# Hash attention and SwiGLU on one core: the normed x of six units turned by DMA instead of on TensorE, with the feed forward planned four slots later

## The chip, the cores and the metric

The kernel runs on one core of a Trainium2 chip. TensorE (PE) multiplies matrices and also transposes blocks by multiplying with an identity; VectorE (DVE), ScalarE (ACT) and GpSimd (POOL) do the rest; SP issues most of the DMAs. Each engine takes its instructions strictly in the order in which the program gives them, and waits for data of other engines through semaphores. The metric is the device time of one execution in microseconds (us). Lower is better.

## The reference

The first half is attention with a hash mask: a query sees the keys whose six sign bits under a fixed projection equal its own. The second half normalises the rows and feeds them through a gated layer.

```python
B, H, S, D = 4, 8, 768, 64            # batch, heads, sequence, head size
mask   = bucket(q @ proj)[:, :, :, None] == bucket(k @ proj)[:, :, None, :]
scores = where(mask, q @ k.T / sqrt(D), -1e9)
attn   = exp(scores - max); attn = attn / (sum(attn) + 1e-09)
x      = (attn @ v).transpose(0, 2, 1, 3).reshape(3072, 512)
rms    = sqrt(mean(x * x, axis=-1) + 1e-06)
xn     = x / rms * rms_g
g, val = xn @ w_gate, xn @ w_val      # 512 -> 1536 each
out    = (g * sigmoid(g) * val) @ w_out   # 1536 -> 512, float32
```

## The kernel before, in words

**Units and slots.** The 3072 rows are cut into eight units of 384 rows: unit u is half u % 2 of batch u // 2. Attention goes through 192 slots. Slot t issues the scores of step t + 1 (`scores`, line 335, two matmuls), the exponential of step t on ACT (`probs`, line 347), and then whatever a plan holds for that slot. Three slots make one head, 24 slots (`NS`) one unit. Scores lie in two PSUM buffers, so the scores of step t + 2 wait until the exponential of step t is done. Two of each three slots also hold half of the product with v (`av`, line 360).

**After a pair of heads**, `o_step` (lines 374 to 387) puts the pair's output in the float32 tile `x` of the unit: an addition and a reciprocal on DVE, a product on POOL. `s_step` (lines 397, 403) adds up the squares. For unit u of 1 to 6, with t0 = 24 (u + 1), the last pair's `o_step` lies in slot t0 + 2, its `s_step` and the norm in slot t0 + 4. `norm_scale` reduces on DVE (415) and takes the power -1/2 on POOL (419), and `norm_third` (430) multiplies each third of `x`, 128 rows by 512, by the row's factor into the fp16 tile `xn`: three DVE instructions.

**Turning.** The feed forward needs xn with the 512 columns on the partitions. `turn_x` does a third: four PE transposes of 128x128 into a PSUM bank (`x_ps`, 437), and one DVE instruction (443) that writes them to `xnT` and multiplies by the norm's weight, which lies along the partitions there (`gcol`). For the last third of unit 0 and the middle one of unit 7, ACT does this in four instructions (441).

**Feed forward.** For each of 12 blocks of 128 hidden columns there are `gate` and `value`, four matmuls of 384 columns each (454), halved into two pieces. ACT takes a tanh of the gate (462), DVE makes two passes (471, 472) and writes `ht`. `project` (483) multiplies `ht` by `wo` into `y_ps`, `store` (495, 496) copies a third of the output on ACT and sends it off on SP's queue. All PSUM banks of this part (`x_ps`, `g_ps`, `v_ps`, `y_ps`, the hash's `d_ps`) come from one pool of three (`bank`).

**The planner.** `spread(t0, n, pieces)` deals pieces of PE work into n slots, so that the estimated PE time (`PROJ` 216 ns, `FEED` 324, `TURN` 220, with fixed amounts for scores and av) is even over the slots. In the window of unit u, slots t0 to t0 + 23, the pieces are, in this order: nine pieces of four `project` matmuls of unit u - 1, with the three turns of unit u behind the seventh and the eighth, and then 48 halves of gate and value of unit u. Unit 0's gates lie in slots 38 to 47. The hash (`hash_one`) and the means of v have slots of their own and take their share of the time.

**The tail.** After slot 191 nothing of scores is left. A few slots finish the last head (av in slots 193 and 194, the last `o_step` on DVE in slot 194), then `project(6, ...)`, norm(7), three `turn_x(7, ...)`, the gates and values of unit 7 and its projections follow without a planner.

SP's queue carries the loads of q, k and v (105, 119), the hash bits (294) and the stores (496). ACT's queue carries two DMAs in all: one at the start (512) and the very last store (508).

## Time and profile before

| | us |
|---|---|
| median of 2 runs | 331.15 (330.91 to 331.39) |
| the profiled execution: time / span on the chip | 330.52 / 328.7 |
| busy: PE / DVE / ACT / POOL | 323.0 / 239.5 / 227.2 / 158.4 |
| granted TensorE clock | 0.999 |

The span runs from the first to the last instruction; the 1.8 us by which the time exceeds it lie around the program. A busy engine is one that executes instructions; time in which it waits is idle. Instructions that issue a DMA are not counted as busy; they stand in the trace under the engine's queue (SPq, ACTq), with the time that they hold the issuing sequencer. PE's matmuls overlap in the records, so the cost of a PE instruction is read from the distance between the starts of neighbours, not from its own duration.

### The profile page before, as it was taken

The page shows a single profiled execution, that of the slowest core. Times are in us where ns is not written, and L with a number is a line of the kernel's source. Part 1 is how long each engine was busy: PE and PEld are TensorE (multiplying, and loading weights), DVE is VectorE, ACT ScalarE, POOL GpSimd, SP SyncE. Part 2 cuts the span into 40 slices and gives each one's busy share as a digit, 9 for nine tenths or more (in the row PEclk, how much of TensorE's full clock was granted, in tenths as well). Part 3 has the DMA queues.
Part 4 walks back from the last instruction along what each step waited for, and adds up shares of the span by engine and source line. Part 5 has one row for each costly group of instructions (what it writes and reads, how often), then busy time and mean ns, then how long its engine had stood idle before and what let it go on. Part 6 is the DMA issues. An engine that isn't in the chain of part 4 may idle for free.

```text
span 328.7 us, 7869 instructions
## 1 busy us (share of the span) xinstructions
PE 323.0 (98%) x2999; PEld 196.6 (60%) x2999; DVE 239.5 (73%) x526; ACT 227.2 (69%) x331; POOL 158.4 (48%) x204
## 2 busy tenths in 40 slices
PE   8999999999999999999999999999999999999995
PEld 3676666656565566656566565655566566665554
DVE  5887877859888778967888568876768455685860
ACT  7999886766678677775768667785767767744321
POOL 4999759955974542824674521755462111221000
PEclk9999999999999999999999999999999999999999
DMA  7943999988139554432816136001000010002002
GB/s 236 335 158 99 225 211 191 184 157 142 70 58 165 118 114 87 73 77 82 164 21 133 36 93 117 7 3 68 34 5 3 34 64 2 0 2 96 3 1 97
DMA packets 79614, 30.93 MB, mean 94 GB/s; under 512 B 64908, under 2 KB 76632, under 8 KB 79576
## 3 DMA queue, kind: packets, MB, share of 16 engines
q1 hardware_dynamic: 75672, 25.65, 33.2%
q0 software_dynamic: 3680, 4.72, 8.5%
q8 instruction: 23, 0.38, 0.5%
q14 instruction: 15, 0.12, 0.1%
q10 hardware_dynamic: 224, 0.07, 0.1%
HBM read 28.32 MB, written 6.29 MB: 105 GB/s over the span
## 4 chain that ended last, share of the span: by engine, by line
PE 97%; ACT 1%; issue 0%; DVE 0%
PE s_ps L335 20%; PE g_ps L454 19%; PE v_ps L454 19%; PE y_ps L483 18%; PE o_ps L360 11%; PE d_ps L215 2%; PE t_ps L155 2%; PE d_ps L235 2%; PE x_ps L437 2%; PE z_ps L550 1%; ACT psb L347 1%; PE y_ps L502 1%; PE m_ps L319 1%; DVE kT L157 0%; PE s_ps L155 0%
## 5 line engine op out<-in xcount | busy, mean ns | idle before, releaser
L347 ACT ACTIVATE psb<-s_ps,ebias 128x768 f16<-128x768 f32 x192 | 167.7, 899 | 20.8 <-PE s_ps L335 19.9
L335 PE MATMUL s_ps<-QK 128*128 128x384 f16 (+1 forms) x384 | 93.5, 326 | 1.2 <-ACT psb L347 1.1
L462 ACT ACTIVATE t<-g_ps 128x384 f32<-128x384 f32 x96 | 47.1, 491 | 53.0 <-PE g_ps L454 52.9
L454 PE MATMUL g_ps<-xnT,wg 128*128 128x384 f16 x384 | 82.6, 326 | 0.0
L454 PE MATMUL v_ps<-xnT,wv 128*128 128x384 f16 x384 | 81.8, 326 | 0.0
L471 DVE SCALAR_TENSOR_TENSOR a<-t,g_ps 128x384 f32<-128x384 f32 x96 | 52.9, 551 | 27.6 <-ACT t L462 26.0
L381 POOL TENSOR_TENSOR x<-otmp,rcp 128x384 f32<-128x384 f32 x30 | 25.1, 835 | 95.5 <-DVE rcp L379 95.3
L483 PE MATMUL y_ps<-wo,ht 128*128 128x512 f16 x276 | 68.0, 379 | 0.0
L472 DVE SCALAR_TENSOR_TENSOR ht<-a,v_ps 128x384 f16<-128x384 f32 x96 | 53.2, 554 | 11.2 <-PE v_ps L454 2.9
L360 PEld LDWEIGHTS <-psb 128*128 128x128 f16 x1152 | 51.9, 97 | 15.7 <-issue 1.2
L360 PE MATMUL o_ps<-vl,psb 128*128 128x65 f16 x1152 | 55.8, 193 | 0.0
L335 PEld LDWEIGHTS <-QK 128*128 128x128 f16 (+1 forms) x384 | 34.6, 98 | 34.3 <-issue 9.2
L454 PEld LDWEIGHTS <-wv 128*128 128x128 f16 x384 | 35.3, 97 | 21.2 <-issue 0.2
L454 PEld LDWEIGHTS <-wg 128*128 128x128 f16 x384 | 34.8, 97 | 20.8 <-DVE xnT L443 0.4
L483 PEld LDWEIGHTS <-ht 128*128 128x128 f16 x276 | 24.8, 98 | 22.4
L495 ACT COPY ysb<-y_ps 128x512 f32<-128x512 f32 x23 | 13.5, 585 | 19.6 <-PE y_ps L483 19.6
L374 DVE TENSOR_TENSOR otmp<-o_ps,cvb 128x390 f32<-128x390 f32 x32 | 17.8, 557 | 7.6 <-PE o_ps L360 7.6
L207 POOL CAST QK<-qT 64x768 f16<-64x768 f32 x20 | 16.4, 820 | 13.4 <-DVE qT L194 12.8
L430 DVE TENSOR_SCALAR xn<-x,rstd 128x512 f16<-128x512 f32 x23 | 15.8, 738 | 6.8 <-POOL rstd L419 6.8
L387 POOL TENSOR_TENSOR sq<-x 128x384 f32<-128x384 f32 x24 | 19.8, 826 | 1.9
L443 DVE TENSOR_TENSOR xnT<-x_ps,gcol 128x512 f16<-128x512 f16 x22 | 14.5, 686 | 8.0 <-PE x_ps L437 7.9
L207 POOL CAST QK<-kT 64x768 f16<-64x768 f32 x20 | 16.4, 820 | 6.6 <-DVE kT L194 4.7
(83 smaller groups left out, 284.5 us busy)
## 6 DMA issues: line engine op xcount, KB each, us to landing
vn<-in_v_dram SPq DMA_DIRECT2D x16, 384.0 KB
out_dram<-ysb SPq DMA_DIRECT2D x23, 256.0 KB
qL<-in_q_dram SPq DMA_DIRECT2D x40, 96.0 KB
kL<-in_k_dram SPq DMA_DIRECT2D x40, 96.0 KB
kn<-in_k_dram SPq DMA_DIRECT2D x5, 384.0 KB
qn<-in_q_dram SPq DMA_DIRECT2D x5, 384.0 KB
wg<-in_moe_w_gate_dram POOLq DMA_DIRECT2D x2, 768.0 KB, 9.7
wv<-in_moe_w_val_dram POOLq DMA_DIRECT2D x2, 768.0 KB, 11.8
```

Source lines behind the costliest of these rows:

```text
L207: nc.gpsimd.tensor_copy(QK[b, 2 * hp + hh, "h"][0:64, o : o + S], src[64 * hh : 64 * hh + 64, :])
L335: nc.tensor.matmul(ps[:, j, 0:HALF], QK[b, h, "h"][rows, S + jt * 128 : S + (jt + 1) * 128], QK[b, h, "h"][rows, half * HALF : (half + 1) ...
L347: nc.scalar.activation(psb[u, h][:, 2 * ch : 2 * ch + 2, :], sps.pop((u, i))[:, :, 0:HALF], AF.Exp, bias=ebias, scale=ESCALE,)
L360: nc.tensor.matmul(o[:, c, hh, 0:65], psb[u, h][:, jt, c * 128 : (c + 1) * 128], vls[b % 2][:, h, 2 * (jt % 3) + jt // 3 if b in PARITY el ...
L374: nc.vector.tensor_add(tmp[:, :, :, 0:65], o[:, :, :, 0:65], cvb[b % 2][:, 2 * hp : 2 * hp + 2, 0:65].unsqueeze(1).to_broadcast([128, 3, 2 ...
L381: eng.tensor_mul(xd.rearrange("p c (h d) -> p c h d", h=2), tmp[:, :, :, 0:64], r.to_broadcast([128, 3, 2, 64]),)
L387: eng.tensor_mul(sq, xd, xd)
L454: nc.tensor.matmul(ps, w[:, kt, fs], xnT[u][:, kt, :], start=(kt == 0), stop=(kt == 3))
L462: nc.scalar.activation(t, fbank[u, ft, "g_ps"], AF.Tanh, scale=0.5)
L471: nc.vector.scalar_tensor_tensor(out=a, in0=t, scalar=1.0, in1=g, op0=ALU.add, op1=ALU.mult)
L472: nc.vector.scalar_tensor_tensor(out=ht[u][:, ft, :], in0=a, scalar=0.5, in1=vv, op0=ALU.mult, op1=ALU.mult)
L483: nc.tensor.matmul(y, ht[u][:, ft, c * 128 : (c + 1) * 128], wo[:, ft, :], start=(ft == 0), stop=(ft == NF - 1),)
```

## The change

For units 1 to 6 the turn leaves PE. The norm's third becomes one DVE instruction with two tensor operands, which multiplies x by the row's factor and by the norm's weight, laid out along the columns in a new tile `grow` that every partition holds in full. Then `turn_dma` has ACT's queue issue a DMA that transposes the third from `xn` into `xnT`. The three DMAs of a unit lie in slots t0 + 6, t0 + 7 and t0 + 8, behind the exponential of that slot on ACT. `grow` is loaded in slot 3 by SP (one row of 2 KB read for each of 128 partitions) and scaled in slot 41 by ACT. Units 0 and 7 keep `turn_x`.

The planner's windows move by `LAG` = 4 slots: unit 0's gates have slots 38 to 51, and the window of unit u is t0 + 4 to t0 + 27. The window of unit 6 thus ends at slot 195, four slots behind the last scores. The norm's slot does not move.

```diff
+    grow = const.tile([128, DMODEL], FP32, name="grow")
...
+    ONDMA = range(1, 7)
+
+    def turn_dma(u, c):
+        if c == 0:
+            xnT[u] = npool.tile([128, 4, HALF], FP16, name="xnT", bufs=2)
+        nc.scalar.dma_start_transpose(
+            out=xnT[u][:, :, c * 128 : (c + 1) * 128], in_=xn[u][:, c, :]
+        )
...
         for c in range(3 if u else 2):
-            norm_third(u, c, nc.vector.tensor_scalar_mul)
+            if u in ONDMA:
+                nc.vector.scalar_tensor_tensor(
+                    out=xn[u][:, c, :], in0=x[u][:, c, :], scalar=rstds[u][:, c : c + 1],
+                    in1=grow, op0=ALU.mult, op1=ALU.mult,
+                )
+            else:
+                norm_third(u, c, nc.vector.tensor_scalar_mul)
...
+    at(0, 3, nc.sync.dma_start, grow, moe_rms_g.partition_broadcast(128))
+    at(0, 41, nc.scalar.mul, grow, grow, float(DMODEL) ** 0.5)
...
+    LAG = 4
...
-            spread(t0, 2 * NS - t0, gates)
+            spread(t0, 2 * NS + LAG - t0, gates)
             continue
         t0 = NS * (u + 1)
         at(0, t0 + 4, norm, u)
+        for c, s in enumerate((6, 7, 8)):
+            at(0, t0 + s, turn_dma, u, c)
...
-            if i in (6, 7):
-                pieces += [
-                    (TURN, False, [(0, turn_x, u, c)]) for c in ((0,), (1, 2))[i - 6]
-                ]
-        spread(t0, NS, pieces + gates)
+        spread(t0 + LAG, NS, pieces + gates)
```

More of the change, by code (lines that the diff above doesn't have):

```diff
@@ L737 @@
         at(0, t, idle_bank, n)
-    SCORES, AV, PROJ, FEED, TURN, HASH, MEAN = 330, 290, 216, 324, 220, 1000, 120
+    SCORES, AV, PROJ, FEED, HASH, MEAN = 330, 290, 216, 324, 1000, 120
     inserts = {spot[3]: (HASH, hash_one, *pair) for pair, spot in spots.items()}
```

## The prediction

> **What bounds the kernel now.** I read the page's first part, then the chain that ended last, then the stages around the norm of units 1 to 6, one window from slot t0 + 6 on for each, and last the tail.

> ```profile
> PE 323.0 (98%) x2999; PEld 196.6 (60%) x2999; DVE 239.5 (73%) x526; ACT 227.2 (69%) x331; POOL 158.4 (48%) x204
> PE 97%; ACT 1%; issue 0%; DVE 0%
> 73.90:81.00 7.10, 7.10 (x64) 4.36 (x62) 6.95 (x12) 4.79 (x7) 3.26 (x6) 1.00 0.96 164
> 112.00:119.00 7.00, 7.00 (x63) 4.27 (x62) 4.60 (x8) 4.84 (x8) 3.15 (x5) 1.00 0.25 94
> 265.00:272.00 7.00, 6.93 (x69) 4.29 (x68) 3.85 (x7) 4.75 (x7) 1.59 (x2) 1.00 0.19 75
> ```

> The windows' columns are length, then busy PE, PEld, DVE, ACT and POOL, the granted clock, the DMA share and GB/s. PE is busy throughout at full clock, so work taken from PE there shortens the kernel as long as nothing new makes PE wait. ACT has some 2.2 us free in 7. In unit 1's window (73.9) DVE and the DMA engines are nearly full; there the change has least room. The timeline shows the step itself, for unit 2 (slot t0 + 4 starts at 109.32, with the scores that PE issues in it):

> ```profile
> 109.32 0.49 PE L335 MATMUL s_ps<-QK 128*128 128x384 f16 x2
> ...
> 110.03 0.86 POOL L419 TENSOR_TENSOR rstd<-ss,mhalf 128x3 f32<-128x3 f32 x1 [1.05 <-DVE ss L415]
> 110.92 2.76 DVE L430 TENSOR_SCALAR xn<-x,rstd 128x512 f16<-128x512 f32 x3 [0.97 <-POOL rstd L419]
> 111.37 0.90 ACT L347 ACTIVATE psb<-s_ps,ebias 128x768 f16<-128x768 f32 x1 [0.62 <-PE s_ps L335]
> 113.44 0.39 PE L437 MATMUL x_ps<-ident,xn 128*128 128x128 f16 x4
> 113.66 1.03 PE L483 MATMUL y_ps<-wo,ht 128*128 128x512 f16 x4
> 113.86 0.69 DVE L443 TENSOR_TENSOR xnT<-x_ps,gcol 128x512 f16<-128x512 f16 x1 [0.18 <-PE x_ps L437]
> ```

> **What goes.** The four transposes start at 113.44 and the next matmul at 113.66: 0.22 us of PE for a third (0.23 in the tail, 298.96 to 299.19). Eighteen thirds at 0.225 are **-4.05 us**, all on the path. Eighteen evictions at 0.69, 12.4 us, leave DVE; DVE isn't the bound, so I count nothing for them, nor for the three-bank pool having a user less.

> **What comes on DVE.** The third was 0.48 us where POOL is quiet and up to 1.22 beside POOL's casts and additions. No two-operand pass of 512 columns is in the trace. The nearest row is the product x<-otmp,rcp on DVE, 384 columns from two SBUF tensors, 0.557; the 128 further columns add what separates 384 (0.554, L472) from 512 (0.69, L443), so 0.69. Bounds 0.48 to 1.22; a unit's three take 2.1 where they took 1.45 to 2.9. Nothing on the path.

> **What comes on ACT's queue.** Eighteen DMA issues. ACT takes nothing behind one until it is issued, and a DMA waits for its third of xn. Behind it stand the exponentials, and PE's scores wait for those. What an issue costs for a transpose no row shows; rows of issues in the trace:

> ```profile
> L508 ACTq DMA_DIRECT2D out_dram<-ypart x1: 354/354/354, 325.6 to 325.6; - x1
> L512 ACTq DMA_DIRECT2D praw<-in_proj_dram x1: 554/554/554, 0.7 to 0.7; - x1
> L294 SPq DMA_DIRECT2D QK<-bits x80: 659/667/1319, 78.1 to 244.5; - x80
> L119 SPq DMA_DIRECT2D qL<-in_q_dram x40: 561/644/5683, 37.3 to 196.2; - x40
> ```

> (ns: least, median, most.) I call the issue I, from 0.35 to 5.7 us, and take **0.67**, the hash bits, the only transfer from SBUF to SBUF.

> When is the third there? Times are us after the start of slot t0 + 4. Now rstd starts between 0.0 and 1.6. After the change the last gate and value of the unit before lie in slot t0 + 3, so DVE still owes two passes of 0.55 behind a tanh when the slot starts: about 1.3. Then the squares (three of 0.22), the reduction (0.17), the power (0.86): xn's thirds at about 3.8, 4.5 and 5.2, an estimate from these rows. ACT ends the exponential of t0 + 6 at about 2.95 (112.27 in unit 2), so the first DMA waits 0.85 and ends at 3.8 + I. The exponential of t0 + 7 starts at 3.6 now, so it is 0.2 + I late. By the gap in the trace between an exponential's end and the scores that need its buffer, it may be 1.06 to 2.1 late, by unit. With I = 0.67 PE loses nothing. The second and third DMAs end at 3.8 + 2I and 3.8 + 3I where I is above 0.7; the exponentials behind them start at some 5.6 and 7.1 now and have 1.1 to 1.9 and 1.5 to spare. So a unit's stall begins between I = 0.9 and 1.6 and then grows as **3I - 4.8**.

> Landing: PE's first gate of the unit comes behind all nine project pieces: 9 x 0.864, seven scores of 0.325 and nearly five av halves of 0.29, so 11.4. The nearest transfers: the first k tile (192 KB) is issued at 0.73 and used at 3.37, 2.6 us; the last store (64 KB) starts at 325.61 and the span ends at 328.74, 3.1. The last third, issued at 5.2, lands by 5.9 + 3 = 8.9 (I = 0.67), 2.5 before its use. **Nothing**; it costs from a landing of 5.6 us up. POOL's 768 KB loads (9.4 to 11.8) are the upper bound.

> [...] No run here shows a transposing DMA yet.

> **grow.** Its load adds 256 KB behind loads needed much later; nothing. Its scaling is one ACT pass (0.73, L430 on ACT) in a gate slot, where the exponential has 0.5 to spare: **+0.2**.

> **The lag.** It takes no work away, so it matters only where PE's covers change. In slots 38 to 51 PE has less per slot (1.6 us against 2.07); POOL, 16.1 of 16.8 us busy from 47.9 to 64.7, doesn't shrink with it, and may bring x of unit 1 late: **+0.3**. The tail is worse:

> ```profile
> 294.04 0.55 DVE L374 TENSOR_TENSOR otmp<-o_ps,cvb 128x390 f32<-128x390 f32 x1
> ...
> 296.20 0.17 DVE L415 TENSOR_REDUCE ss<-ssp 128x3 f32<-128x15 f32 x1
> 296.46 0.85 POOL L419 TENSOR_TENSOR rstd<-ss,mhalf 128x3 f32<-128x3 f32 x1 [5.53 <-DVE ss L415]
> ```

> Here the last o_step holds DVE 2.13 us (294.04 to 296.17) beside PE's projections of unit 6, which ask nothing new of DVE. With the lag, gates and values 10 and 11 of unit 6 stand around that o_step in slots 194 and 195. PE does value 10 and gate 11 (0.65 each) and then needs a third bank for value 11, the one of gate 10, which DVE frees only behind the o_step and its own pass: 2.13 + 0.55 against 1.3, so **+1.45**. The norm of unit 7 then comes at 5.9 to 6.7, ahead of the turns at 9.5.

> **Sum.** -4.05 + 0.2 + 0.3 + 1.45 = -2.1 us. The profiled execution's 330.52 (span 328.7) becomes 328.4; it lay 0.6 under the median, so **329.0**, for which I give 0.52 (326.7 to 331).

> **Rivals.**
> - *ACT's issue takes the place of PE's turn* (slower). All six units pay 3I - 4.8. It eats the gain at I = 1.7 and makes 2% at about 2.1; I = 2 gives 336, 2.5 gives 345. For it: the qL issues that took up to 5.7 us with the queue loaded, and 0.55 for 1.5 KB on ACT when SP issued in the same instant, against 0.35 alone. Against: medians under 0.7, and SP's string of bits stands behind the norm (unit 1, from 78.06). [...] 0.22.
> - *The landing is late*, PE's first gate waits. Each us beyond 5.6 costs 6: 7 us give 337, 9.4 give 352. For it: 96% DMA share in unit 1's window; against: 0.19 to 0.55 in the other five. 0.14.
> - *The tail costs nothing*, and the evictions' absence helps: -4.05, 327.0, or 326 with a us of small stalls gone. 0.08.
> - *The DMA does not turn in blocks* but moves 2-byte elements: a packet costs 23 ns (33.2% of 16 engines' 328.7 us over 75672), 65536 of them over 16 engines 94 us a third; far over 400. 0.04.

> **Range and chances.** What a measurement tells from no change is about 2%, 324.5 to 337.8 here. Faster than that needs more than the whole PE gain: 0.02. Slower: two thirds of the ACT rival, half of the landing's, the last: 0.26. The rest, 0.72, is same. 326.5 to 341 leaves out the upper ends of both slow rivals and little below.

> **What would show it.** Right: x_ps for units 0 and 7 alone (24 transposes); ACTq issues under a us; no idle of PE at scores or first gates in the six windows; a wait of about 1.4 us of PE on DVE's pass 471 before value 11 near the end. Wrong: PE waiting for psb (ACT rival), or gates waiting on the xnT DMA (landing). The weakest step is I, taken from a plain copy.

## The result and the profile after

| | before | after |
|---|---|---|
| median of 2 runs, us | 331.15 (330.91 to 331.39) | 355.85 (355.66 to 356.04) |
| span of the profiled execution, us | 328.7 | 353.8 |
| granted TensorE clock | 0.999 | 0.981 |

The changed kernel takes 1.0745 times as long (95% interval 1.0727 to 1.0762): 24.7 us more where 2 us less were forecast, and far above the range. The page of the changed kernel, its busy times, the granted clock by slices, and the chain that ended last:

```profile
PE 328.9 (93%) x2926; PEld 194.5 (55%) x2927; DVE 232.5 (66%) x508; ACT 226.6 (64%) x332; POOL 161.3 (46%) x204
...
PEclk9999999996999999999978999999999999999999
...
PE 66%; DVE 11%; POOL 8%; ACT 4%; DMA 3%; issue 3%; SPq 2%; ACTq 1%; DVEq 0%; POOLq 0%
```

PE was 97% of the chain and is 66% now. PE has become busier in spite of 72 transposes less, and the clock line says why: the granted clock is 0.6 in one slice of the span and 0.7 and 0.8 in two neighbouring ones further on. What PE waits for is in its list of waits (engine, line, what it waited for: us in total, times, longest):

```profile
PE s_ps L336 <- DMA QK<-bits: 11.1, 2, 6.5
PE s_ps L336 <- ACT psb L348: 5.6, 12, 1.2
PE v_ps L470 <- DVE a L487: 1.9, 2, 1.6
```

The largest wait is for the hash bits. The change doesn't touch these: they come from the hash through DVE and are sent to their place by SP's queue. Before, no scores waited for them. The waits for exponentials are short, twelve of 0.5 us on average, and the third line is mostly the tail. PE's timeline has the two long waits (start, duration, instruction; in brackets the idle time before it and what ended it):

```profile
84.28 0.80 PE L336 MATMUL s_ps<-QK 128*128 128x384 f16 x2 [4.56 <-DMA QK<-bits]
...
183.07 0.80 PE L336 MATMUL s_ps<-QK 128*128 128x384 f16 x2 [6.51 <-DMA QK<-bits]
```

They are the first scores of the pairs (batch 1, pair 2) and (batch 2, pair 3), steps 60 and 114. The windows of the changed kernel behind them (columns as in the prediction's windows) show that the matter doesn't end with the wait:

```profile
84.20:91.50 7.30, 7.22 (x42) 3.87 (x43) 1.11 (x2) 2.79 (x5) 6.04 (x6) 0.62 0.31 114
91.50:100.00 8.50, 8.50 (x79) 4.97 (x78) 7.04 (x15) 6.00 (x9) 1.66 (x2) 1.00 0.02 5
183.00:190.00 7.00, 6.93 (x41) 3.88 (x42) 2.79 (x6) 2.06 (x4) 0.00 (x0) 0.59 0.44 70
```

In the 7 us behind each wait PE is fully busy, but at 0.62 and 0.59 of its clock, and does 42 and 41 matmuls, where the 8.5 us from 91.5 on, at full clock, hold 79. The clock's records put both stretches at half speed for 6.83 us, from 82.93 and from 181.92, while PE was still idle. Before, where PE has no such wait, they have full speed from 3.65 us to 327.91.

**Why the bits are late.** SP's timeline around the second wait, before:

```profile
136.99 2.65 SPq L119 DMA_DIRECT2D kL<-in_k_dram  x4
...
145.49 5.97 SPq L294 DMA_DIRECT2D QK<-bits  x8
...
164.20 5.98 SPq L294 DMA_DIRECT2D QK<-bits  x8
```

and after:

```profile
145.00 17.43 SPq L120 DMA_DIRECT2D kL<-in_k_dram  x4
...
163.32 7.30 SPq L295 DMA_DIRECT2D QK<-bits  x8
170.66 2.98 SPq L120 DMA_DIRECT2D qL<-in_q_dram  x4
173.75 2.64 SPq L120 DMA_DIRECT2D kL<-in_k_dram  x4
176.49 0.59 SPq L106 DMA_DIRECT2D vn<-in_v_dram  x1
177.19 1.42 SPq L512 DMA_DIRECT2D out_dram<-ysb  x3
178.69 5.97 SPq L295 DMA_DIRECT2D QK<-bits  x8
```

Four loads of a k tile, 2.65 us before, hold SP's queue for 17.4. Then SP issues without a pause and can't catch up: the bits for step 114 are issued at 178.69 in place of 164.20, 14.5 us late, and step 114 comes at 183.07 in place of 169.06, 14.0 late. What SP waited for in the changed kernel:

```profile
SPq L120 <- DMA xnT<-xn: 18.5, 2, 14.9
SPq L295 <- DMA xnT<-xn: 10.8, 4, 8.6
```

| issued at, us | DMA | its semaphore | who had it last, landed at |
|---|---|---|---|
| 144.25 | SP `qL<-in_q_dram`, the fourth | 100 | |
| 145.00 | SP `kL<-in_k_dram` | 104 | |
| 145.63 | SP `kL<-in_k_dram` | 105 | |
| 146.32 | SP `kL<-in_k_dram` | 106 | |
| 159.42 | ACT `xnT<-xn` | 107 | |
| 160.83 | ACT `xnT<-xn` | 109 | |
| 161.87 | SP `kL<-in_k_dram` | 107 | ACT's of 159.42, 161.85 |
| 162.18 | ACT `xnT<-xn` | 103 | |
| 162.53 | SP `vn<-in_v_dram` | 108 | |
| 163.32 | SP `QK<-bits` | 109 | ACT's of 160.83, 163.26 |
| 164.13 | SP `QK<-bits` | 100 | |
| 166.28 | SP `QK<-bits` | 103 | ACT's of 162.18, 166.22 |

So the fourth load of k waits for unit 3's first transpose and the bits for the second and third, and each is issued 0.02 to 0.06 us after the landing. SP reached that place at 147; ACT could issue these transposes only when the norm had made xn, at 159.42, 160.83 and 162.18. A DMA that waits on ACT's queue thus holds SP's queue, 12 us before it is issued itself. Each unit has such a place: unit 1's transposes hold loads of pair (2,0) at 71.66, in front of the bits of step 60 (issued at 81.34, before at 78.06).

**The transposes themselves.** Rows of the timeline for unit 2, whose slot t0 + 4 starts at 114.38 (to be held against the one shown of before):

```profile
116.96 0.86 POOL L429 TENSOR_TENSOR rstd<-ss,mhalf 128x3 f32<-128x3 f32 x1 [1.45 <-DVE ss L425]
117.85 3.56 DVE L438 SCALAR_TENSOR_TENSOR xn<-x,rstd,grow 128x512 f16<-128x512 f32 x3 [0.97 <-POOL rstd L429]
118.56 1.44 POOL L310 TENSOR_TENSOR vadd<-vn 128x384 f32<-128x384 f32 x1
119.18 1.21 ACTq L418 DMA_TRANSPOSE xnT<-xn  x1
120.43 0.90 ACT L348 ACTIVATE psb<-s_ps,ebias 128x768 f16<-128x768 f32 x1 [3.16 <-PE s_ps L336]
120.58 1.20 ACTq L418 DMA_TRANSPOSE xnT<-xn  x1
121.38 0.48 PE L336 MATMUL s_ps<-QK 128*128 128x384 f16 x2 [0.40 <-ACT psb L348]
121.94 1.50 ACTq L418 DMA_TRANSPOSE xnT<-xn  x1
123.27 0.48 PE L336 MATMUL s_ps<-QK 128*128 128x384 f16 x2 [0.27 <-ACT psb L348]
```

The thirds of xn are there 4.8, 6.2 and 7.0 us after the slot's start. ACT stands before the first DMA until then, the exponentials behind it are late, and PE's scores wait 0.3 to 0.4 us for them. (The row at 120.43 puts ACT's idle time down to PE's scores; what ended last was the issue from 119.18 on, which holds ACT to 120.39.) The groups of the new instructions (the first: least, median and most ns; the second: busy us, mean ns, then its idle time):

```profile
L418 ACTq DMA_TRANSPOSE xnT<-xn x18: 1203/1206/1502, 72.8 to 288.0; - x18
L438 DVE SCALAR_TENSOR_TENSOR xn<-x,rstd,grow 128x512 f16<-128x512 f32 x18 | 18.4, 1075 | 5.9 <-POOL rstd L429 5.9
```

**Where the span went.** PE's time, taken from the distances between the starts of neighbouring matmuls (162 ns for an undisturbed one of 384 columns, 216 for 512, 29 for 65, 56 for a transpose; what is above goes to the wait, or, inside a stretch at half clock, to the half clock). Two of the experiments stand beside it:

| us | before | lag alone | units 2, 4, 5, 6 by DMA | after |
|---|---|---|---|---|
| undisturbed work | 299.07 | 299.07 | 296.38 | 294.83 |
| hash matmuls with their waits | 14.09 | 15.36 | 18.10 | 17.03 |
| scores waiting for bits or exponentials | 0 | 1.55 | 5.64 | 18.36 |
| added by the half clock | 0 | 0 | 0 | 5.43 |
| values waiting for a bank, tail included | 0.16 | 5.17 | 5.08 | 2.26 |
| the rest (start, end, small gaps) | 15.42 | 15.59 | 15.02 | 15.93 |
| span | 328.74 | 336.74 | 340.22 | 353.84 |

The trace of the changed kernel lacks the record of one matmul (2926 in place of 2927), so 0.21 us of its undisturbed work stand in another row: 72 transposes at 56 ns are 4.03 us, not the 4.24 between the columns.

### The profile page after: what moved, and what is told of

Its sections match the earlier page's. It is cut to its first block, busy times and chain, and to the rows that moved or that the text cites. A ratio compares the mean times of both kernels' runs of the same rounds, so it can differ in the third digit from the quotient of the medians.

```text
span 353.8 us, 7741 instructions
## 1 busy us (share of the span) xinstructions
PE 328.9 (93%) x2926; PEld 194.5 (55%) x2927; DVE 232.5 (66%) x508; ACT 226.6 (64%) x332; POOL 161.3 (46%) x204
## 4 chain that ended last, share of the span: by engine, by line
PE 66%; DVE 11%; POOL 8%; ACT 4%; DMA 3%; issue 3%; SPq 2%; ACTq 1%; DVEq 0%; POOLq 0%
PE g_ps L470 14%; PE s_ps L336 14%; PE v_ps L470 13%; PE y_ps L499 9%; PE o_ps L361 7%; PE t_ps L156 2%; ACT psb L348 2%; DVE xn L438 2%; DVE a L487 2%; PE d_ps L236 2%; DVE otmp L375 2%; DMA QK<-bits 2%; POOL QK L146 1%; POOL QK L208 1%; PE d_ps L216 1%
## 5 line engine op out<-in xcount | busy, mean ns | idle before, releaser
L336 PE MATMUL s_ps<-QK 128*128 128x384 f16 (+1 forms) x384 | 94.8, 330 | 17.2 <-DMA QK<-bits 11.1
L470 PE MATMUL g_ps<-xnT,wg 128*128 128x384 f16 x384 | 84.7, 331 | 0.2
L499 PE MATMUL y_ps<-wo,ht 128*128 128x512 f16 x276 | 69.0, 382 | 0.0
L470 PEld LDWEIGHTS <-wv 128*128 128x128 f16 x384 | 36.2, 99 | 24.9 <-issue 3.7
L438 DVE SCALAR_TENSOR_TENSOR xn<-x,rstd,grow 128x512 f16<-128x512 f32 x18 | 18.4, 1075 | 5.9 <-POOL rstd L429 5.9
L429 POOL TENSOR_TENSOR rstd<-ss,mhalf 128x3 f32<-128x3 f32 x8 | 6.9, 866 | 21.5 <-DVE ss L425 20.9
```

The source lines that it names most:

```text
L336: nc.tensor.matmul(ps[:, j, 0:HALF], QK[b, h, "h"][rows, S + jt * 128 : S + (jt + 1) * 128], QK[b, h, "h"][rows, half * HALF : (half + 1) ...
L438: nc.vector.scalar_tensor_tensor(out=xn[u][:, c, :], in0=x[u][:, c, :], scalar=rstds[u][:, c : c + 1], in1=grow, op0=ALU.mult, op1=ALU.mult,)
L470: nc.tensor.matmul(ps, w[:, kt, fs], xnT[u][:, kt, :], start=(kt == 0), stop=(kt == 3))
L499: nc.tensor.matmul(y, ht[u][:, ft, c * 128 : (c + 1) * 128], wo[:, ft, :], start=(ft == 0), stop=(ft == NF - 1),)
```

## The experiments

Times are medians; ratios are to the kernel before on the same chip (331.2 to 331.4), with 95% intervals.

### The lag without the transposes

The kernel before with the planner's windows moved, all turns on PE:

```diff
+    LAG = 4
...
-            spread(t0, 2 * NS - t0, gates)
+            spread(t0, 2 * NS + LAG - t0, gates)
...
-        spread(t0, NS, pieces + gates)
+        spread(t0 + LAG, NS, pieces + gates)
```

> The kernel before with the lag of four slots alone; the turns stay on PE. Three theories of the 25 us, from the trace after. A, shared completion semaphores: every DMA of SP's and ACT's queues takes the next of eight semaphores and first waits for the landing of the DMA that had it last, so SP's loads and hash bits wait for the transposes; the scores of slots 59 and 115 then wait 4.7 and 6.7 us for the bits, and PE runs at half clock for 6.8 us behind each, about 18 us in all. B, ACT's issues: each holds ACT's queue 1.2 us, and the wait for xn stands in front; about 7 us of PE waiting at scores in the six windows. C, the lag: moving the feed forward makes the bits, the norm or the tail late by itself. A and B expect 332.5 to 333.5 here (the tail's 1.5 and little else, no wait for bits). C expects over 340.

Measured: 338.62 us (337.64 to 339.14), ratio 1.0219 (1.0194 to 1.0245). This is more than two of the theories said and less than the third: the lag alone costs 7.4 us. The waits of PE in this kernel:

```profile
PE v_ps L454 <- DVE a L471: 4.0, 7, 1.6
PE s_ps L335 <- DMA QK<-bits: 1.3, 1, 1.3
```

In the table above, 5.0 of the 8.0 us of its span are values that wait for a bank of the gate until DVE's pass has freed it: 1.79 in the tail and 3.2 spread over the windows. Scores of step 60 waiting for bits take 1.5, the hash 1.3. Nothing but the plan's order differs from the kernel before, so each of these is a wait that the old order covered and the moved one doesn't.

### The transposes without the lag, and without a reader

The kernel before in full; ACT issues the same eighteen transposes besides, into a tile that nothing reads:

```diff
+    scr = const.tile([128, 4, HALF], FP16, name="scr")
...
+    def turn_scratch(u, c):
+        nc.scalar.dma_start_transpose(
+            out=scr[:, :, c * 128 : (c + 1) * 128], in_=xn[u][:, c, :]
+        )
...
+        for c, s in enumerate((6, 7, 8)):
+            at(0, t0 + s, turn_scratch, u, c)
```

> The kernel before, with no lag and with the turns on PE, plus the 18 transposing DMAs from xn on ACT's queue in slots t0 + 6 to t0 + 8, into a scratch tile that nobody reads. A expects SP's queue to wait for the transposes of units 1 and 3 as after the change, the scores to wait for bits, and 343 to 352. B alone expects 332 to 338 (xn is ready earlier than with the lag) and no wait for bits. C expects 331 to 332.

Measured: 344.48 us (342.86 to 346.09), ratio 1.0400 (1.0340 to 1.0459). The waits of PE:

```profile
PE s_ps L336 <- DMA QK<-bits: 9.1, 3, 5.9
PE x_ps L438 <- ACT ysb L501: 1.6, 2, 1.2
```

Nothing depends on these DMAs, nothing on PE has moved, and the same two scores (87.03 and 182.21 here) wait for bits, with some 3.6 us lost at half clock behind. These make up most of the 13 us; they are the coupling through SP's queue without the lag. The turns' wait for ACT's copy (1.6) comes on top: ACT stands before the DMAs here too.

### Two kilobytes in place of 128

The same places, but a plain copy of eight rows of 256 B:

```diff
-        nc.scalar.dma_start_transpose(
-            out=scr[:, :, c * 128 : (c + 1) * 128], in_=xn[u][:, c, :]
+        nc.scalar.dma_start(
+            out=scr[0:8, 0, c * 128 : (c + 1) * 128], in_=xn[u][0:8, c, 0:128]
```

> The kernel before, its turns on PE and its planner unmoved, plus eighteen plain DMAs on ACT's queue in slots t0 + 6 to t0 + 8 of units 1 to 6. Each copies eight rows of 256 B (2 KB) from the third of xn into a tile that nothing reads, so next to no data moves and nothing transposes; only the places in the order of the DMAs and the wait for xn stay as with the turned thirds. A (hardware DMAs of SP and ACT share a few completion signals in turn, and each DMA waits for the landing of the one that had its signal before): SP's loads and hash bits still wait for these landings, PE's scores again wait 5 us or more in all for hash bits, as with the whole transposes (344.5), 339 to 346. B (the data, or ACT's 1.2 us per transposing issue): 331 to 333, no wait of scores for bits.

Measured: 338.78 us (338.28 to 341.3), ratio 1.0241 (1.0202 to 1.0280). The time lies just under the lower end of theory A and far from B. SP's timeline of this kernel still has the held loads of k, and PE waits for bits:

```profile
141.73 16.40 SPq L120 DMA_DIRECT2D kL<-in_k_dram  x4
```

```profile
PE s_ps L336 <- DMA QK<-bits: 6.3, 2, 4.7
```

So 36 KB in all, in DMAs that nobody reads, cost 7.4 us. It is the place in the order and the wait for xn, not the data. (The lines are of the slowest of the four executions, 341.3; the other three took 338.3 to 338.8.) The whole transposes cost 5.7 more; how that divides between their longer landing and the issue wasn't measured.

### Only four units by DMA

The changed kernel with units 1 and 3, whose transposes stood ahead of the two long waits, turned on PE as before:

```diff
-    ONDMA = range(1, 7)
+    ONDMA = (2, 4, 5, 6)
...
+            if u in ONDMA:
+                at(0, t0 + s, turn_dma, u, c)
...
+            if i in (6, 7) and u not in ONDMA:
+                pieces += [
+                    (220, False, [(0, turn_x, u, c)]) for c in ((0,), (1, 2))[i - 6]
+                ]
```

> The changed kernel, lag included, but units 1 and 3 turn on PE as before; the DMAs turn units 2, 4, 5 and 6. These two units' transposes are those that SP's queue waited for ahead of the late bits. A expects both long waits for bits and the half clock behind them to go: 355.9 - 18 + 1.35 for the turns on PE - 2 for two units' waits at ACT, 336 to 338. B expects only its two units' share: 354 to 355. C expects 355 to 357.

Measured: 341.0 us (339.71 to 342.3), ratio 1.0295 (1.0246 to 1.0344): 3 us above A's range, far below the others. Two units less by DMA save 14.9 us: both long waits and all of the half clock are gone, and the loads of k at that place take 3.89 us. A held DMA of SP with slack behind it costs little: here SP still stands before a load of v for 10.9 us, to 117.67, until a transpose has landed, and no long wait of PE follows. The rest over the kernel before is the lag, and 3.7 us of short waits for exponentials. What A left out is in the table: without the long waits, values wait 2.8 us more for banks than in the changed kernel, and the hash takes 1.1 more.

### The transposes on SP's queue

```diff
-        nc.scalar.dma_start_transpose(
+        nc.sync.dma_start_transpose(
```

> The changed kernel with the transposes issued from SP's queue instead of ACT's, in the same slots. Nothing of ACT waits for xn or for an issue any more, and SP comes to the bits in the order of the slots, not ahead of the norm. A and B both expect no wait for bits at slots 59 and 115 and no wait at scores for exponentials: 328.5 to 332 (PE's 4.05 less, the tail's 1.8 more, some landing). C expects 345 or more. If the landing is late, the first gate of a unit waits: 332 to 336.

Measured: 353.1 us (352.53 to 354.82), ratio 1.0669 (1.0639 to 1.0699): a miss, in the range of C, though C's waits aren't what the trace shows. But for one wait of 1.7 us for bits, bits and exponentials are on time. The transposes, though, stand behind loads and bits in SP's own order: unit 1's thirds are ready at 74.7 to 77.0, and their DMAs are issued at 85.48 to 88.84, behind eight bits from 79.62 on. The first gates of units 1 and 3 wait for them:

```profile
PE g_ps L470 <- DMA xnT<-xn: 14.1, 2, 7.2
```

So in this order the transposes are held in place of the bits.

### A source that is ready

The changed kernel; the DMAs read a part of `wv`, which is in place long before, so that ACT doesn't wait for the norm (the feed forward of units 1 to 6 then computes with these weights in place of xn):

```diff
-            out=xnT[u][:, :, c * 128 : (c + 1) * 128], in_=xn[u][:, c, :]
+            out=xnT[u][:, :, c * 128 : (c + 1) * 128], in_=wv[:, c, 0:DMODEL]
```

> The changed kernel, but each transposing DMA reads a part of the weight tile that lies ready long before, not xn (what the feed forward computes is another thing then; the work is the same). No DMA on ACT's queue waits for the norm any more; the issue of 1.2 us and the shared completion semaphores stay. In the ledger of PE's starts the changed kernel has 11.3 us at scores behind projections, 6.6 of it short waits in the six windows. If the wait for xn on ACT's queue is what makes the exponentials late, these 6.6 fall below 2. If the issue does it, 4 or more stay. The waits for bits shrink by what SP no longer waits, 2 to 8 us. 336 to 346 for the first, 343 to 350 for the second.

Measured: 347.55 us (347.06 to 348.04), ratio 1.0488 (1.0462 to 1.0514). By its time alone this is the second theory's range and 1.5 us above the first's. The waits of PE decide for the first as to the exponentials, and show what it had wrong, the bits:

```profile
PE s_ps L336 <- DMA QK<-bits: 9.8, 2, 5.5
...
PE s_ps L336 <- ACT psb L348: 1.1, 2, 0.8
```

The two waits for exponentials of 1.1 us in all lie near the start of the kernel and are in the kernel before too; the ten in the six windows are gone, although ACT still issues eighteen transposes of 1.2 us. So it is ACT's standing before xn that delays the exponentials, not the issue, as the first theory had it. The waits for bits stay nearly whole: ACT reaches unit 3's first DMA at 155.0, and SP stands at its k loads from 143.1 on, so the difference in place is enough for them.

### A copy in place of the transpose

```diff
-        nc.scalar.dma_start_transpose(
-            out=xnT[u][:, :, c * 128 : (c + 1) * 128], in_=xn[u][:, c, :]
+        nc.scalar.dma_start(
+            out=xnT[u][:, :, c * 128 : (c + 1) * 128],
+            in_=xn[u][:, c, :].rearrange("p (k n) -> p k n", k=4),
```

The columns then aren't turned, and the feed forward computes with another matrix.

> The changed kernel with a plain DMA copy of the same 128 KB in place of each transpose, on the same queue in the same slots (the columns are not turned, so what is computed is another thing; the work is the same). Every semaphore stays as it was. If the shared semaphores and the wait for xn carry the loss, it stays: 345 to 355, with bits late at slots 59 and 115; the issue shrinks from 1.2 to about 0.5 us and takes 2 to 4 us off the short waits. If transposing itself slows the other transfers, it falls below 340.

Measured: 350.77 us (349.53 to 352.01), ratio 1.0585 (1.0538 to 1.0633). An issue is 0.60 us in place of 1.21, and the waits for exponentials shrink; the bits are as late as before (9.7 us of waits). Transposing isn't the cause.

### The same copy on POOL's queue

POOL's DMAs take their semaphores from another set: in the traces before and after, its six raise 111 to 116, and none of SP's or ACT's does. As with the copy on ACT's queue, the feed forward gets columns that aren't turned.

```diff
-        nc.scalar.dma_start(
+        nc.gpsimd.dma_start(
```

> The changed kernel with plain copies in place of the transposes (the feed forward gets columns that are not turned), issued by POOL's queue in place of ACT's. With the same copies on ACT's queue it took 350.8. A (shared completion signals of the queues of SP and ACT): POOL's DMAs have signals of their own, so SP's hash bits are on time, PE has no wait of over 2 us for them and no half clock behind; what is left is the lag (338.6) less the turns (4.2): 333 to 338, or up to 341 if POOL, held behind the DMA until xn is there, is late with its casts and products. B (the DMA traffic or the moved plan makes the bits late): 347 to 353, the two long waits stay.

Measured: 339.01 us (337.16 to 341.31), ratio 1.0236 (1.0187 to 1.0285): 11.8 us less than with the same copies on ACT's queue, inside the wider of theory A's ranges. Some of it is ACT's: the waits for exponentials are 2.2 us there and 1.1 here. SP's loads of k at the place in question take what they took before:

```profile
139.50 2.65 SPq L120 DMA_DIRECT2D kL<-in_k_dram  x4
```

Step 114 comes without a wait. But one wait for bits is left that A didn't expect, 3.3 us at step 60 (82.11), with a short half clock behind it. There SP is early (bits issued at 77.43, before at 78.06), and PE arrives at 78.6. Before, step 60 ran at 82.33 without a wait, with bits issued at nearly the same time. With the lag alone it waits for its bits until 81.25, with four units by DMA until 82.55. So these bits are there at 81 to 82.5 even where no DMA holds SP, and PE's old work, turns included, just covered them.

### The change without its lag

```diff
-    LAG = 4
+    LAG = 0
...
-        for c, s in enumerate((6, 7, 8)):
+        for c, s in enumerate((6, 7, 7)):
```

> The changed kernel with the lag set to 0; the third DMA moves from slot t0 + 8 to t0 + 7, so that it stands ahead of the gates that read it. xn comes earlier (2.6 to 5.3 us after slot t0 + 4 in the trace before), so ACT hardly waits for it, and the lag's own 7.4 us go; the gates come at about 7 us, the third should land at 6.5 to 8. From the scratch run, 344.5, less 4.2 for the turns on PE: 339 to 342, with the waits for bits and the half clock as in scratch, if landing costs nothing. If the landing is late, 1 to 3 us more in each unit: 345 to 358.

Measured: 354.68 us (353.48 to 355.88), ratio 1.0703 (1.0657 to 1.0749), in the range given for a late landing. The first gates of all six units wait for the landing, 1.2 to 3.6 us each and some 15 in all, and the half clock adds some 8. So the lag does hide the landing, at a price of its own.

> As nolag, but units 1 and 3 turn on PE as before. Shared semaphores: no late bits, no half clock, no lag; 331.2 less 2.7 for twelve turns on PE, plus short waits at ACT: 328.5 to 331, the only version that could beat the kernel before. If ACT's issues or late landings carry weight of their own, 332 to 338.

(No lag, units 1 and 3 on PE.) Measured: 342.52 us (342.36 to 343.23), ratio 1.0335 (1.0317 to 1.0352): a miss, above both ranges. No bits are late, but gates wait for landings in all four units, 9.3 us in all, and one stretch of 3.41 us runs at half clock.

### Shorter lags for four units

Units 1 and 3 on PE, `LAG = 1`, then `LAG = 3`:

> The changed kernel with units 1 and 3 turned on PE and the feed forward moved by one slot in place of four. Without any lag the first gates waited 2.1 to 2.9 us for the landing in each of the four units; one slot is about 1.7 us. If the cost of the lag is in proportion to its slots (7.4 for four): 331.2 - 2.7 + 4 x 0.8 + 1.9 = 333.6; range 331 to 336. If the bank waits of the values and the late bits of slot 59 come with any lag at all: 337 to 341.

Measured: 339.78 us (339.5 to 340.03), ratio 1.0256 (1.0241 to 1.0271): outside the range given, and in that of its rival, but not for the rival's reason: no scores wait for bits, and values wait 0.7 us. Gates still wait for landings, 1.2 to 1.7 us in units 2, 5 and 6, and in unit 1 for its turn on PE.

> The same with the feed forward moved by three slots: no gate waits for a landing. In proportion: 331.2 - 2.7 + 5.6 + 2 to 3.7 for the short waits of scores for exponentials = 336 to 338. If the cost of the lag does not fall with its slots: 340 to 342, as with four.

Measured: 337.35 us (336.44 to 338.03), ratio 1.0174 (1.0154 to 1.0193). The number is that of the proportion, but in part by luck: scores wait for exponentials only 0.5 us more than before, not 2 to 3.7, and the hash matmuls with their waits take 20.1 us in place of 14.1. This is the best of the versions with transposing DMAs, 18.5 us under the changed kernel and still 6 over the one before. No version beat that.

## Why the prediction was wrong

**The step that failed: "What comes on ACT's queue."** It names what stands behind a DMA on ACT, the exponentials, and stops there. SP's queue, which waits for these DMAs by the shared semaphores, isn't in the sum nor in any rival; SP's string of bits is named only as an argument against a slow issue. Taking units 1 and 3 off the DMA gave back 14.9 of the 24.7 us, the bits and the half clock behind them. Eighteen DMAs that nobody reads, added to the kernel before, cost 13.3 us with 128 KB and 7.4 with 2 KB each; copies on a queue outside the rotation cost 11.8 less than the same copies on ACT's. No price of a term would have caught it: the wait lies on an engine that the change doesn't touch, for data that the engine doesn't use.

**"The lag. It takes no work away, so it matters only where PE's covers change."** The sentence holds, its size doesn't: +0.3 and +1.45 stood for it, and alone it costs 7.4. The tail was right in place and size: 1.79 against 1.45, on DVE's pass a. With the lag alone, the same bank wait occurs all along the windows (3.2), where the prediction looked for it only in the tail; bits at step 60 (1.5) and waits around the hash matmuls (1.3) come on top.

**xn's readiness.** Thirds at 3.8, 4.5 and 5.2 were forecast; 4.2 to 5.1, 4.9 to 6.5 and 5.5 to 7.4 came. The passes were sized at 0.69: they take 0.75 in units 4 and 6, and up to 1.49 in the others, where POOL has casts and additions beside them; the bounds were 0.48 and 1.22. And the reduction ends 2.5 us after the slot's start in unit 2, where 2.1 was forecast. The stall of ACT that follows is the mechanism of the rival "ACT's issue", but by the wait for xn: 6.6 us of scores in six windows.

**I, called the weakest step.** It is 1.2 us, not 0.67, and did no harm: 3I - 4.8 is below zero there, and the run with a ready source, with the same issues, has no such stall.

**Right:** the work taken from PE, -4.05 forecast, and 72 transposes of 56 ns less in the trace, 4.03; only units 0 and 7 turn on PE (24 transposes left); the landing in time. In the DMA records the last data of a third land 2.0 us after the start of its issue where nothing else is under way (119.18 to 121.15) and at most 2.9 us after it for any of the eighteen, so the 3 us assumed held for the data; the semaphores tell the landing 2.4 to 4.0 us after it, and no gate of PE waits for it. `grow` shows no cost, where 0.2 was forecast: up to 42 us, PE is idle 2.06 us with it and 1.95 in the lag alone, without it; from 42 to 70 us, where it is scaled (50.3), 0.26 in both.

**What stays open.** The transposes of units 1 and 3 were taken off together, so their shares aren't separated by a run. A transposing DMA with a semaphore of its own wasn't tried. POOL's queue took copies only.

## What to carry to other kernels

A DMA that stood early in the order but waited long for its data wasn't private to its queue here: SP's loads of k waited 18.5 us and its bits 10.8 for transposes of ACT's queue. Ask which later DMAs of other queues wait for its completion, read that from their semaphores, and put such a DMA behind those whose landing is due soon, or on a queue that doesn't share (POOL's, with the copies: 11.8 us less). A plan moved by a few slots is a new plan: each bank and buffer that just came free in time has to be looked at again, not the ends of the move alone. Work taken off the busiest engine is no gain where something else, here the hash bits at step 60, was due at the same moment.

## What the runs showed of the hardware that was not expected

- Between its first matmul and its last, PE is idle for more than a microsecond four times in the changed kernel: 4.56 us from 79.72, 6.51 from 176.56, 1.16 from 248.74 and 1.63 from 316.02. The clock's records have half speed for 6.83 us from 82.93 and from 181.92, which is 3.21 us into the first of these and 5.36 into the second, and full speed around the other two. Before, PE is never idle for a microsecond. What sets the half clock off isn't shown by this.
- Behind the wait of 4.56 us, which ends at 84.28, 5.5 us of the half clock are left, in which PE loses 2.7.
- The issue of a transposing DMA of 128 x 512 fp16 held ACT's sequencer for 1.206 us (the median of the eighteen), that of a plain copy of the same 128 KB 0.602.
- The pass with two float32 tensors, 128 x 512, took 0.75 us with POOL quiet (units 4 and 6) and up to 1.49 beside POOL's casts and additions.
